# Top-k attention and a gated feed-forward on one core: 144 equal units, one tail transpose, a new order within a unit

## The chip, the cores and the metric

One core of a Trainium2 chip runs the whole program. Times are microseconds on the device, from one execution or, where it is said, the median of several; lower is better. PE is TensorE, DVE is VectorE, ACT is ScalarE, POOL is GpSimd, SP is SyncE, which issues the transfers.

## What is computed

```python
# q, k, v: (8, 8, 576, 64) float32: batch, heads, sequence, head width
scores = (1 / sqrt(64)) * q @ k.transpose(0, 1, 3, 2)
kth = the 32nd largest of each row
scores = where(scores >= kth, scores, -1e9)
attn = exp(scores - max); attn = attn / (sum(attn) + 1e-9)
x = (attn @ v) as 4608 rows of 512
h = x @ w_in                # (4608, 2048)
out = (h * cos(h)) @ w_out  # (4608, 512)
```

All of it is float32. The weights arrive as float64 and are decoded on the chip.

## The kernel before

**Units.** The work of attention is cut into units: one tile of queries of one batch with one pair of heads (`hp`, four pairs). A sequence has 576 rows, four tiles of 128 and a tail of 64. A full unit has 128 queries for each of its two heads, so two score tiles of 128 x 576. A tail unit has 64 queries, and its two heads share the partitions of one tile. There are 128 full and 32 tail units (lines 134 to 143).

**Stages of a unit.** `scores` (L173) multiplies q and k on PE, in two halves of 288 keys for each head, and ACT copies them to `s`. `topk_round` (L201), four times on DVE, takes the eight largest (MAX8) and blots them out (MATCH_REPLACE8). `bounds` (L217, POOL) makes the two limits, `softmax` (L231, ACT) a Prelu that sinks what is below the 32nd value and an Exp that sums into `den`; `reciprocal` (L246) adds epsilon on POOL and divides on DVE; `normalise` (L255) multiplies on POOL. `transpose_main` (L263) turns four tiles of 128 keys for each head, `transpose_tail` (L278) the last 64 keys of each head, with a copy by ACT behind each. `values` (L290) is P@V on PE, the tail's matmul of 64 rows last, and a copy to `xT`.

**Feed-forward.** When all units of a block of tokens are done (256 tokens, 128 at both ends; 20 blocks), `ff1` (L335) multiplies by `w_in` into PSUM, ACT copies to `g`, POOL reduces to one period in four passes (L360 to L363), ACT takes the sine (L373), POOL multiplies (L379), and `ff2` (L382) multiplies by `w_out`. A chunk is a tile of 1,024 columns of `g`; five of them exist (`CHUNKS`).

**The order.** The loop at L445 writes slot i with the top-k of unit i, the softmax of unit i - 1 and the transposes and P@V of unit i - 2; the scores of unit i + 2 are asked for first. `feed` (L404) puts in pieces of the feed-forward by a credit of 2.1 per full unit, at most 4 stored, the second product first if its chunk is gated. A call of `ff1` issues 2,048 moved columns on PE, and one of `ff2` also. A scheduler then orders each engine's instructions by their dependences, so that the rows of an engine need not stand as the code is written. The weights are decoded in the first eight slots, four chunks of 128 x 512 in each.

Of the kernel before, what the change touches and what calls it, by code (L numbers as in the profile page):

```python
# [30 lines left out]
def kernel(  # L31
# [58 lines left out]
    stages = ExitStack()  # L90
    staged = {}

    def load_weights(i):
# [6 lines left out]
        st = stage.tile([P, CW, 2], I32, tag="st", name="st")  # L100
        nc.sync.dma_start(out=st.rearrange("p w i -> p (w i)"), in_=src)
        staged[i] = st

    def decode_weights(i):
# [7 lines left out]
        r = stage.tile([P, CW], I32, tag="lo", name="lo")  # L112
        nc.scalar.mul(out=r, in_=lo.bitcast(U32), mul=2.0**-29)
        sg = stage.tile([P, CW], F32, tag="sg", name="sg")
# [20 lines left out]
    for b in range(B):  # L135
        if b % 2 == 0:
            tiles = [(i * P, P) for i in range(NT)] + [(MAIN, TAIL)]
        else:
            tiles = [(0, TAIL)] + [(TAIL + i * P, P) for i in range(NT)]
        for q0, rows in tiles:  # L140
            for hp in range(NP):
                units.append({"b": b, "hp": hp, "q0": q0, "rows": rows, "tok": b * S + q0})
    NU = len(units)
    pairs = {}

    def load_qk(b, hp):
        if b >= B:
            return
        st = pairs[b, hp] = {}
        for name, src in (("q", qT), ("k", kT)):  # L150
            t = loads.tile([P, S], F32, tag=name, name=name)
            nc.sync.dma_start(
                out=t, in_=src[b, 2 * hp : 2 * hp + 2].rearrange("h d s -> (h d) s")
            )
            st[name] = t

    def load_v(b, hp):
        if b >= B:
            return
        st = pairs[b, hp]  # L160
# [4 lines left out]
        t = loads.tile([TAIL, P], F32, tag="v_tail", name="v_tail", bufs=6)  # L165
        nc.sync.dma_start(out=t, in_=v[b, MAIN:S, cols])
        st["v_tail"] = t

    def head_rows(u, j):
        r0 = j * (P - u["rows"])  # L170
        return slice(r0, r0 + u["rows"])

    def scores(u):  # L173
        st = pairs[u["b"], u["hp"]]
        qs = slice(u["q0"], u["q0"] + u["rows"])
        sc = ps.tile([P, 2, 2, 512], F32, tag="sc", name="sc", bufs=1)
        for h in range(2):
            for j in range(2):
                d = slice(j * D, (j + 1) * D)
                nc.tensor.matmul(  # L180
                    sc[head_rows(u, j), j, h, 0:HS],
                    st["q"][d, qs],
                    st["k"][d, h * HS : (h + 1) * HS],
                    start=True,
                    stop=True,
                )
        s = work.tile([P, 2, S], F32, tag="s", name="s", bufs=5)
        u["s"], u["n"] = s, u["rows"] * 2 // P
        if u["n"] == 2:
            nc.scalar.copy(  # L190
                out=s.rearrange("p j (h w) -> p (j h) w", h=2),
                in_=sc.rearrange("p j h w -> p (j h) w")[:, :, 0:HS],
            )
        else:
            for j in range(2):
                r = head_rows(u, j)
                nc.scalar.copy(
                    out=s[r, 0].rearrange("p (h w) -> p h w", h=2), in_=sc[r, j, :, 0:HS]
                )

    def topk_round(u, rnd):  # L201
        s, n = u["s"], u["n"]
# [6 lines left out]
        for j in range(n):  # L209
            nc.vector.max(m8[:, j, at], src[:, j])  # L210
        if rnd < TOPK // 8 - 1:
            for j in range(n):
# [4 lines left out]
    def bounds(u):  # L217

        n = u["n"]
        nb = small.tile([P, 2, 2], F32, tag="nb", name="nb")  # L220
        nc.gpsimd.tensor_scalar(  # L221
            out=nb[:, 0:n], in0=u.pop("m8")[:, 0:n, 0 : TOPK : TOPK - 1], scalar1=-SCALE,
# [3 lines left out]
        nc.gpsimd.tensor_tensor(  # L226
            out=nd[:, 0:n], in0=nb[:, 0:n, 0], in1=nb[:, 0:n, 1], op=ALU.subtract
        )
        u["nb"], u["nd"] = nb, nd

    def softmax(u):  # L231

        s, n, nb, nd = u["s"], u["n"], u.pop("nb"), u.pop("nd")
        for j in range(n):
# [3 lines left out]
        den = small.tile([P, 2], F32, tag="den", name="den")  # L238
        for j in range(n):
# [4 lines left out]
        u["den"] = den  # L244

    def reciprocal(u):  # L246
        n, den = u["n"], u["den"]
        nc.gpsimd.tensor_scalar(  # L248
            out=den[:, 0:n], in0=den[:, 0:n], scalar1=1.0, scalar2=EPS, op0=ALU.mult, op1=ALU.add
        )  # L250
        rden = small.tile([P, 2], F32, tag="rden", name="rden")
        nc.vector.reciprocal(rden[:, 0:n], den[:, 0:n])  # L252
        u["rden"] = rden

    def normalise(u):  # L255
        s, rden = u["s"], u.pop("rden")
        for j in range(u["n"]):
# [5 lines left out]
    def transpose_main(u):  # L263

        s, n = u["s"], u["n"]
        pT = u["pT"] = work.tile([P, NT, 2, P], F32, tag="pT", name="pT")
        for j in range(n):
            tp = ps.tile([P, NT, P], F32, tag="tp", name="tp")
            for c in range(NT):
                nc.tensor.transpose(tp[:, c], s[:, j, c * P : (c + 1) * P], ident)  # L270
            if n == 2:
                nc.scalar.copy(out=pT[:, :, j], in_=tp)  # L272
            else:
                nc.scalar.copy(
                    out=pT[:, :, :, 0:TAIL], in_=tp.rearrange("p c (j s) -> p c j s", j=2)
                )

    def transpose_tail(u):  # L278
        s, n = u["s"], u["n"]
        pt = u["pT_tail"] = work.tile([TAIL, 2, P], F32, tag="pT_tail", name="pT_tail")  # L280
        tp = ps.tile([P, 512], F32, tag="tp", name="tp")
        for j in range(n):
# [258 lines left out]
```

## Time and profile before

| | us |
|---|---|
| median of 3 runs (1915.38 to 1919.62) | 1918.83 |
| the profiled execution's own time | 1908.91 |
| its span, first to last instruction | 1907.1 |
| PE busy | 1708.2 (90%) |
| DVE busy | 1483.7 (78%) |
| ACT busy | 1232.1 (65%) |
| POOL busy | 953.1 (50%) |

The span is that of one execution with the profiler on. A busy share is an average over the decoding at the start, the steady part and the end, in which DVE has nothing to do. A matmul's end is modelled and takes in the drain of the array, so that several that follow each other read as busy although each waits for another engine in between; the distance from start to start tells more. In a row of the timeline the first number is the start, the second the time from there to the end of the last of the xcount instructions merged in it, and the bracket the idle time of the engine before it and what ended that. Each float32 matmul is two rows of the count.

### The profile page before, as it was taken

Reading aid. Unit: us, or ns where it says so; the run is one execution under the profiler, and the core shown is the slowest. Engines: PE = TensorE matmul, PEld = TensorE weight load, DVE = VectorE, ACT = ScalarE, POOL = GpSimd, SP = SyncE. Lnnn points to the kernel's source line nnn. Section 1 sums busy time; section 2 is a strip of 40 time slices with the busy share of each in tenths; the row PEclk is TensorE's granted clock in tenths of the full one; section 3 lists DMA queues with packets and bytes.
Section 4 is the critical chain, followed back from the end, with each engine's and each line's share of the span. In section 5 each row is a group of like instructions: output and inputs, shape, how many; then the busy total and the mean of one; then the engine's idle time right before and its main releaser. Section 6 shows DMA issues by size and latency. Waiting matters only on the chain.

```text
span 1907.1 us, 26842 instructions
## 1 busy us (share of the span) xinstructions
PE 1708.2 (90%) x9632; PEld 1112.8 (58%) x9632; DVE 1483.7 (78%) x3137; ACT 1232.1 (65%) x2146; POOL 953.1 (50%) x1198
## 2 busy tenths in 40 slices
PE   3658999999899999998999999999999999989995
PEld 2346565656565656656565656565656565656653
DVE  7989889986878679897878868988887868897200
ACT  6776776765757575767676766776766666676511
POOL 5895355544545352636363635563635444554613
PEclk9979999999999999999999999999999999999998
DMA  6420110001000010001100010001000010000000
GB/s 220 133 90 16 48 34 7 7 31 37 25 6 1 32 42 25 1 28 35 37 1 12 13 61 13 12 1 62 19 13 6 6 44 19 7 6 6 7 6 11
DMA packets 38598, 56.26 MB, mean 29 GB/s; under 512 B 3136, under 2 KB 21568, under 8 KB 38464
## 3 DMA queue, kind: packets, MB, share of 16 engines
q1 hardware_dynamic: 38464, 54.54, 8.9%
q8 instruction: 76, 1.25, 0.3%
q14 instruction: 58, 0.48, 0.1%
HBM read 45.09 MB, written 9.44 MB: 29 GB/s over the span
## 4 chain that ended last, share of the span: by engine, by line
DVE 26%; PE 25%; POOL 25%; ACT 19%; issue 4%; DMA 0%; POOLq 0%; SPq 0%; ACTq 0%
DVE m L210 13%; DVE rest L213 11%; PE o L391 10%; POOL x L363 7%; PE mm L348 7%; ACT s L240 4%; POOL x L361 3%; POOL s L258 3%; POOL x L362 3%; POOL x L360 3%; PE o L303 3%; ACT s L235 3%; PE sc L180 3%; ACT x L373 3%; POOL g L379 2%
## 5 line engine op out<-in xcount | busy, mean ns | idle before, releaser
L210 DVE MAX8 m<-rest 128x8 f32<-128x576 f32 x864 | 616.1, 747 | 2.9
L348 PE MATMUL mm<-xT,w_in 128*128 128x256 f32 (+1 forms) x2560 | 551.7, 371 | 27.4 <-ACT g L355 13.9
L391 PE MATMUL o<-w_out,g 128*128 128x512 f32 x1152 | 539.9, 612 | 35.8 <-POOL g L379 35.8
L348 PEld LDWEIGHTS mm<-xT,w_in 128*128 128x128 f32 x2560 | 452.0, 197 | 118.9 <-issue 29.0
L213 DVE MATCH_REPLACE8 rest<-m,rest 128x576 f32<-128x576 f32 x576 | 423.8, 742 | 0.0
L391 PEld LDWEIGHTS o<-w_out,g 128*128 128x128 f32 x1152 | 212.4, 194 | 276.8 <-issue 233.7
L210 DVE MAX8 m<-s 128x8 f32<-128x576 f32 x288 | 205.5, 748 | 164.6 <-ACT s L190 136.4
L235 ACT ACTIVATE s<-s,nb 128x576 f32<-128x576 f32 x288 | 215.4, 772 | 153.5 <-POOL nb L221 153.1
L180 PE MATMUL sc<-k,q 64*128 64x288 f32 (+1 forms) x1280 | 270.4, 461 | 21.9 <-ACT s L190 14.1
L258 POOL TENSOR_SCALAR s<-s,rden 128x576 f32<-128x576 f32 x288 | 215.8, 757 | 132.9 <-DVE rden L252 108.1
L240 ACT ACTIVATE s<-s,nd 128x576 f32<-128x576 f32 x288 | 221.8, 771 | 18.3 <-POOL nd L226 16.3
L248 POOL TENSOR_SCALAR den<-den 128x2 f32<-128x2 f32 (+1 forms) x160 | 31.1, 194 | 362.7 <-ACT s L240 353.4
L213 DVE MATCH_REPLACE8 rest<-m,s 128x576 f32<-128x576 f32 x288 | 211.9, 742 | 0.0
L379 POOL TENSOR_TENSOR g<-g,x 128x1024 f32<-128x1024 f32 x72 | 170.1, 2362 | 63.3 <-ACT x L373 62.8
L303 PE MATMUL o<-pT,v 128*64 128x128 f32 (+1 forms) x2560 | 168.5, 276 | 19.6 <-ACT pT L272 12.5
L180 PEld LDWEIGHTS sc<-k,q 64*128 64x128 f32 (+1 forms) x1280 | 128.3, 187 | 87.9 <-issue 31.4
L270 PEld LDWEIGHTS tp<-ident,s 128*128 128x128 f32 x1152 | 136.2, 144 | 70.5 <-issue 38.0
L270 PE MATMUL tp<-ident,s 128*128 128x128 f32 x1152 | 161.1, 280 | 16.6 <-POOL s L258 12.6
L303 PEld LDWEIGHTS o<-pT,v 128*64 128x64 f32 x2560 | 132.0, 141 | 71.5 <-ACT pT L272 30.1
L363 POOL TENSOR_TENSOR x<-g,x 128x1024 f32<-128x1024 f32 x72 | 170.5, 2368 | 1.7
L190 ACT COPY s<-sc 128x1152 f32<-128x1152 f32 x128 | 142.1, 1110 | 38.7 <-PE sc L180 38.4
L272 ACT COPY pT<-tp 128x512 f32<-128x512 f32 x256 | 137.5, 584 | 26.0 <-PE tp L270 25.6
(44 smaller groups left out, 1353.2 us busy)
## 6 DMA issues: line engine op xcount, KB each, us to landing
q<-in_q_dram SPq DMA_DIRECT2D x32, 288.0 KB, 2.8
k<-in_k_dram SPq DMA_DIRECT2D x32, 288.0 KB, 3.2
out_dram<-ob SPq DMA_DIRECT2D x36, 256.0 KB, 2.0
st<-in_moe_w_in_dram SPq DMA_DIRECT2D x16, 512.0 KB, 4.2
v<-in_v_dram SPq DMA_DIRECT2D x32, 256.0 KB, 2.9
st<-in_moe_w_out_dram SPq DMA_DIRECT2D x16, 512.0 KB, 3.5
v_tail<-in_v_dram SPq DMA_DIRECT2D x32, 32.0 KB, 2.6
```

Source lines behind the costliest of these rows:

```text
L180: nc.tensor.matmul(sc[head_rows(u, j), j, h, 0:HS], st["q"][d, qs], st["k"][d, h * HS : (h + 1) * HS], start=True, stop=True,)
L210: nc.vector.max(m8[:, j, at], src[:, j])
L213: nc.vector.match_replace(rest[:, j], m8[:, j, at], src[:, j], NEG)
L235: nc.scalar.activation(out=s[:, j], in_=s[:, j], func=AF.Prelu, bias=nb[:, j, 1:2], scale=SCALE, alpha=FAR)
L240: nc.scalar.activation(out=s[:, j], in_=s[:, j], func=AF.Exp, bias=nd[:, j : j + 1], scale=1.0, accum_out=den[:, j : j + 1],)
L258: nc.gpsimd.tensor_scalar(out=s[:, j], in0=s[:, j], scalar1=rden[:, j : j + 1], scalar2=1.0, op0=ALU.mult, op1=ALU.mult,)
L270: nc.tensor.transpose(tp[:, c], s[:, j, c * P : (c + 1) * P], ident)
L303: nc.tensor.matmul(o[d, 0:w], lhsT, rhs, start=c == 0, stop=c == NT)
L348: nc.tensor.matmul(mm[:, a * w : (a + 1) * w], w_in[f // FC][:, c, (f % FC) * P : (f % FC + 1) * P], blk["xT"][:, c], start=c == 0, stop=c ...
L363: gp.tensor_tensor(out=x, in0=g, in1=x, op=ALU.subtract)
L379: nc.gpsimd.tensor_tensor(out=g, in0=g, in1=x, op=ALU.mult)
L391: nc.tensor.matmul(o, g[:, at : at + P], w_out[f], start=f == 0, stop=f == NF - 1)
```

## The change

**Units** become 144 equal ones of 128 rows of the flattened tokens, each with a list of parts: where a tile straddles two batches (4 tiles, 16 units) scores and P@V are issued once for each part. **The last keys of both heads**: k of the second head is loaded turned by 64 keys (its last 64 first), so that the first head's last 64 columns and the second head's first 64 lie side by side in `s`; one transpose of 128 columns turns both, one copy takes them, and v's tail is a 128 x 128 tile with one head's rows in each diagonal quarter and zeros elsewhere. **The order of a slot**: P@V comes before the scores of unit i + 2, both after the third round; the reciprocal stands behind the fourth round, its epsilon behind the second; normalising moves to the next slot's start. **Feed-forward pieces** are half as large (a call of `ff1` or `ff2` issues 1,024 moved columns), with a credit of 4.2 per unit, at most 6 stored. **Staging** of the weights uses the buffers of the feed-forward. **Loads** are issued at slots worked out from each buffer's last use. **At the end**, when no unit is left (`ff["end"]`), DVE reduces to one period in two passes and multiplies by the sine.

```diff
+    for t0 in range(0, B * S, P):
+        parts = []
+        for i, a in enumerate((t0, t0 + TAIL)):
+            b, q0 = a // S, a % S
+            if parts and parts[-1][0] == b:
+                parts[-1][2] = P
+            else:
+                parts.append([b, q0, TAIL, i * TAIL])
...
+        nc.sync.dma_start(out=t[0:D], in_=kT[b, 2 * hp])
+        nc.sync.dma_start(out=t[D:P, TAIL:S], in_=kT[b, 2 * hp + 1, :, 0:MAIN])
+        nc.sync.dma_start(out=t[D:P, 0:TAIL], in_=kT[b, 2 * hp + 1, :, MAIN:S])
...
+                k0 = j * TAIL + c * P
+                nc.tensor.transpose(tp[:, c], s[:, j, k0 : k0 + P], ident)
...
+        s = u.pop("s").rearrange("p j k -> p (j k)")
+        nc.tensor.transpose(tp[:, 0:P], s[:, MAIN : MAIN + P], ident)
+        nc.scalar.copy(out=pt, in_=tp[:, 0:P])
...
+        if ff["end"]:
+            nc.vector.tensor_scalar(
+                out=x, in0=g, scalar1=0.25, scalar2=MAGIC, op0=ALU.add, op1=ALU.add
+            )
+            nc.vector.scalar_tensor_tensor(
+                out=x, in0=x, scalar=MAGIC, in1=g, op0=ALU.subtract, op1=ALU.subtract
+            )
+            waiting.append((blk, g, x, ff["now"], -TWO_PI_BELOW))
+            return
...
+            eng = nc.vector if ff["end"] else nc.gpsimd
+            eng.tensor_tensor(out=g, in0=g, in1=x, op=ALU.mult)
...
-        for f in range(f0, f0 + 4):
+        for f in range(f0, f0 + 2):
...
+        ff["credit"] = min(ff["credit"] + 4.2, 6.0)
         ff["now"] += 1
-        if i + 2 < NU:
-            scores(units[i + 2])
         if w:
             bounds(w)
-        gates()
+        if x:
+            normalise(x)
         if u:
             topk_round(u, 0)
         decode(1)
         if w:
             softmax(w)
-        sines(2)
-        if credit >= 1 and feed():
-            credit -= 1
+        gates()
+        feed(2)
+        if x:
+            transpose_main(x)
         if u:
             topk_round(u, 1)
         decode(1)
+        feed(1)
+        if x:
+            transpose_tail(x)
+        feed(6)
         if w:
-            reciprocal(w)
-            normalise(w)
+            add_eps(w)
+        sines(2)
         if u:
             topk_round(u, 2)
         decode(1)
         if x:
-            transpose_main(x)
-        while credit >= 1 and feed():
-            credit -= 1
-        if x:
-            transpose_tail(x)
             values(x)
+        if i + 2 < NU:
+            scores(units[i + 2])
         if u:
             topk_round(u, 3)
+        if w:
+            reciprocal(w)
         decode(1)
```

PE, a steady unit before (`mm` first product, `tp` transposes, `o` P@V, `sc` scores):

```order
L348 MATMUL mm<-xT,w_in_80 128x256 x8
L270 MATMUL tp<-ident,s 128x128 x8
L348 MATMUL mm<-xT,w_in_80 128x256 x8
L283 MATMUL tp<-ident,s 64x128 x2
L303 MATMUL o<-pT,v 64x128 x8
L303 MATMUL o<-pT_tail,v_tail 64x128 x2
L180 MATMUL sc<-k,q 128x288 x4
```

and in the changed program a unit with four pieces, then one with half a piece (`o_6591` is the second product's):

```order
L334 MATMUL mm<-xT,w_in_81 128x256 x8
L264 MATMUL tp<-ident,s 128x128 x8
L334 MATMUL mm<-xT,w_in_82 128x256 x4
L272 MATMUL tp<-ident,s 128x128
L334 MATMUL mm<-xT,w_in_82 128x256 x4
L289 MATMUL o<-pT,v 64x128 x8
L289 MATMUL o<-pT_tail,v_tail_112 64x128 x2
L184 MATMUL sc<-k,q 128x288 x4
```

```order
L264 MATMUL tp<-ident,s 128x128 x8
L391 MATMUL o_6591<-w_out_96,g 128x512
L272 MATMUL tp<-ident,s 128x128
L184 MATMUL sc<-k,q 128x288
L289 MATMUL o<-pT,v 64x128 x8
L289 MATMUL o<-pT_tail,v_tail_106 64x128 x2
```

Half of a feed-forward block that stood between transposes and tail now stands between the tail and P@V; the second piece shows a unit in which the feed had almost nothing to give.

DVE, a steady unit, before and in the changed program (`m` the largest values, `rest` what is left of the scores):

```order
L210 MAX m_4286<-s 128x8 x2
L213 MATCH_REPLACE rest<-m_4286,s 128x576 x2
L210 MAX m_4286<-rest 128x8 x2
L213 MATCH_REPLACE rest<-m_4286,rest 128x576 x2
L252 RECIPROCAL rden<-den 128x2
L210 MAX m_4286<-rest 128x8 x2
L213 MATCH_REPLACE rest<-m_4286,rest 128x576 x2
L210 MAX m_4286<-rest 128x8 x2
```

```order
L206 MAX m_4448<-s 128x8 x2
L209 MATCH_REPLACE rest<-m_4448,s 128x576 x2
L206 MAX m_4448<-rest 128x8 x2
L209 MATCH_REPLACE rest<-m_4448,rest 128x576 x2
L206 MAX m_4448<-rest 128x8 x2
L209 MATCH_REPLACE rest<-m_4448,rest 128x576 x2
L206 MAX m_4448<-rest 128x8 x2
L246 RECIPROCAL rden<-den 128x2
```

The reciprocal has moved from between two rounds to the end of the unit.

DVE at the end of the changed program, behind the last top-k, the first two of eleven chunks:

```order
L206 MAX m_12781<-rest 128x8 x2
L246 RECIPROCAL rden<-den 128x2 x2
L350 TENSOR_SCALAR x<-g 128x1024
L353 SCALAR_TENSOR_TENSOR x<-x,g 128x1024
L379 TENSOR_TENSOR g<-g,x 128x1024
L350 TENSOR_SCALAR x<-g 128x1024
L353 SCALAR_TENSOR_TENSOR x<-x,g 128x1024
L379 TENSOR_TENSOR g<-g,x 128x1024
```

Before, these passes stood on POOL, five to a chunk, for all 72 chunks.

## Rows read from the trace of the kernel before

**Rows 1.** The page, busy time of each engine, share of the span, instructions.

```profile
PE 1708.2 (90%) x9632; PEld 1112.8 (58%) x9632; DVE 1483.7 (78%) x3137; ACT 1232.1 (65%) x2146; POOL 953.1 (50%) x1198
```

**Rows 2.** Timeline of DVE in a steady stretch: first MAX8 of units.

```profile
900.37 1.42 DVE L210 MAX8 m<-s 128x8 f32<-128x576 f32 x2 [4.02 <-ACT s L190]
910.74 1.42 DVE L210 MAX8 m<-s 128x8 f32<-128x576 f32 x2 [0.57 <-ACT s L190]
920.40 1.40 DVE L210 MAX8 m<-s 128x8 f32<-128x576 f32 x2
...
998.01 1.42 DVE L210 MAX8 m<-s 128x8 f32<-128x576 f32 x2 [3.76 <-ACT s L190]
```

**Rows 3.** Groups of DVE from 902 to 998.5: busy, mean ns, idle before, releaser.

```profile
L210 DVE MAX8 m<-s 128x8 f32<-128x576 f32 x15 | 10.7, 750 | 11.6 <-ACT s L190 11.6
L252 DVE RECIPROCAL rden<-den 128x2 f32<-128x2 f32 x8 | 1.3, 160 | 7.4 <-POOL den L248 7.4
```

**Rows 4.** Timeline of PE, matmuls, 1738 to 1755.

```profile
1738.39 0.38 PE L283 MATMUL tp<-ident,s 128*64 128x128 f32 x2
1738.70 1.09 PE L303 MATMUL o<-pT,v 128*64 128x128 f32 x16
1739.72 0.44 PE L303 MATMUL o<-pT_tail,v_tail 64*64 64x128 f32 x4
1740.09 1.24 PE L180 MATMUL sc<-k,q 64*128 64x288 f32 x8
1741.26 3.72 PE L348 MATMUL mm<-xT,w_in 128*128 128x256 f32 x16
1744.82 1.04 PE L270 MATMUL tp<-ident,s 128*128 128x128 f32 x8
1745.69 3.62 PE L348 MATMUL mm<-xT,w_in 128*128 128x256 f32 x16
...
1754.13 0.44 PE L303 MATMUL o<-pT_tail,v_tail 64*64 64x128 f32 x4 [1.82 <-ACT pT_tail L284]
```

**Rows 5.** Groups by form, whole span: waits that the tail units have their share in.

```profile
L210 DVE MAX8 m<-s 128x8 f32<-128x576 f32 x288 | 205.5, 748 | 164.6 <-ACT s L190 136.4 <-ACT s L197 28.2
...
L252 DVE RECIPROCAL rden<-den 128x1 f32<-128x1 f32 x32 | 5.0, 156 | 40.3 <-POOL den L248 40.2
```

**Rows 6.** Timeline of DVE: the ninth unit's first MAX8, the last unit's last.

```profile
146.44 0.76 DVE L210 MAX8 m<-s 128x8 f32<-128x576 f32 x1
...
1778.83 1.41 DVE L210 MAX8 m<-rest 128x8 f32<-128x576 f32 x2
```

**Rows 7.** Stretches: length, busy PE, PEld, DVE, ACT, POOL, granted clock, DMA share, GB/s.

```profile
900.00:998.00 98.00, 92.31 (x499) 60.95 (x498) 78.62 (x168) 64.68 (x112) 47.33 (x60) 0.97 0.06 18
...
1893.50:1904.00 10.50, 9.59 (x16) 3.90 (x16) 0.00 (x0) 0.60 (x1) 0.13 (x1) 0.75 0.00 0
```

**Rows 8.** Timeline of PE at the end, behind the last P@V and the last matmuls.

```profile
1820.04 14.00 PE L391 MATMUL o<-w_out,g 128*128 128x512 f32 x32
...
1893.68 9.59 PE L391 MATMUL o<-w_out,g 128*128 128x512 f32 x16 [10.10 <-POOL g L379]
```

**Rows 9.** Groups by form, whole span: prices of single operations.

```profile
L213 DVE MATCH_REPLACE8 rest<-m,rest 128x576 f32<-128x576 f32 x576 | 423.8, 742 | 0.0
L240 ACT ACTIVATE s<-s,nd 128x576 f32<-128x576 f32 x288 | 221.8, 771 | 18.3 <-POOL nd L226 16.3
L379 POOL TENSOR_TENSOR g<-g,x 128x1024 f32<-128x1024 f32 x72 | 170.1, 2362 | 63.3 <-ACT x L373 62.8
L373 ACT ACT_TABLE_LOAD x67 | 86.0, 1283 | 1.2
L355 ACT ACTIVATE g<-mm 128x512 f32<-128x512 f32 x144 | 84.2, 586 | 100.4 <-PE mm L348 100.3
L373 ACT ACTIVATE x<-x,halfpi 128x1024 f32<-128x1024 f32 x72 | 82.7, 1148 | 86.4 <-POOL x L363 86.2
L119 DVE TENSOR_SCALAR w_in<-w_in x16: 401/417/761, 12.2 to 72.0; 128x512 f32<-128x512 f32 x16
```

More of the change, by code (lines that the diff above doesn't have):

```diff
@@ L179, in scores @@
                 d = slice(j * D, (j + 1) * D)
[L180 to L199, printed above, removed]
+                for b, q0, rows, r0 in u["parts"]:
+                    st = pairs[b, u["hp"]]
+                    nc.tensor.matmul(
+                        sc[r0 : r0 + rows, j, h, 0:HS],
+                        st["q"][d, q0 : q0 + rows],
+                        st["k"][d, h * HS : (h + 1) * HS],
+                        start=True,
+                        stop=True,
+                    )
+        s = u["s"] = work.tile([P, 2, S], F32, tag="s", name="s", bufs=5)
+        nc.scalar.copy(
+            out=s.rearrange("p j (h w) -> p (j h) w", h=2),
+            in_=sc.rearrange("p j h w -> p (j h) w")[:, :, 0:HS],
+        )
     def topk_round(u, rnd):
-        s, n = u["s"], u["n"]
+        s = u["s"]
         if rnd == 0:
@@ L237, in softmax @@
             )
-        den = small.tile([P, 2], F32, tag="den", name="den")
-        for j in range(n):
+        den = u["den"] = small.tile([P, 2], F32, tag="den", name="den")
+        for j in range(2):
             nc.scalar.activation(
@@ L243, in softmax, with add_eps @@
             )
-        u["den"] = den
-    def reciprocal(u):
[L247 to L253, printed above, removed]
+    def add_eps(u):
+        den = u["den"]
+        nc.gpsimd.tensor_scalar(
+            out=den, in0=den, scalar1=1.0, scalar2=EPS, op0=ALU.mult, op1=ALU.add
+        )
+    def reciprocal(u):
+        u["rden"] = small.tile([P, 2], F32, tag="rden", name="rden")
+        nc.vector.reciprocal(u["rden"], u.pop("den"))
     def normalise(u):
         s, rden = u["s"], u.pop("rden")
-        for j in range(u["n"]):
+        for j in range(2):
             nc.gpsimd.tensor_scalar(
@@ L263, in transpose_main @@
     def transpose_main(u):
-        s, n = u["s"], u["n"]
+        s = u["s"]
         pT = u["pT"] = work.tile([P, NT, 2, P], F32, tag="pT", name="pT")
-        for j in range(n):
+        for j in range(2):
             tp = ps.tile([P, NT, P], F32, tag="tp", name="tp")
             for c in range(NT):
[L270 to L276, printed above, removed]
+                k0 = j * TAIL + c * P
+                nc.tensor.transpose(tp[:, c], s[:, j, k0 : k0 + P], ident)
+            nc.scalar.copy(out=pT[:, :, j], in_=tp)
@@ L393, in ff2 @@
             )
-        if f0 + 4 < NF:
+        if f0 + 2 < NF:
             return
@@ L441, in decode @@
                 ff["weights"] += 1
-    per_batch = NU // B
-    credit = 0.0
+    last = {}
+    for i, u in enumerate(units):
+        for part in u["parts"]:
+            last[part[0], u["hp"]] = i
+    at_slot = {}
+    order = [(b, hp) for b in range(B) for hp in range(NP)]
+    for load, bufs, behind in ((load_qk, 5, -1), (load_v, 6, 3)):
+        for n in range(NP, len(order)):
+            slot = last[order[n - bufs]] + behind if n >= bufs else 2
+            at_slot.setdefault(slot, []).append((load, *order[n]))
+    load_qk(0, 0)
+    load_weights(0)
+    load_qk(0, 1)
+    load_weights(1)
+    scores(units[0])
+    for hp in range(2, NP):
+        load_qk(0, hp)
+    for hp in range(NP):
+        load_v(0, hp)
+    scores(units[1])
     for i in range(NU + 2):
+        ff["end"] = i >= NU
         u = units[i] if i < NU else None
```

203 lines of the change are left out of this document (83 added, 120 removed).

## The prediction

> **What bounds the kernel now.** I read the shares of busy time first, then the DVE timeline of one steady stretch, then PE's timeline beside it, then the two ends of the program.
>
> The shares say PE 90%, DVE 78% [rows 1], which looks like a matmul-bound kernel. The steady stretch says otherwise. On DVE a unit's top-k that waits for nothing takes 9.66 us from first MAX8 to first MAX8 (910.74 to 920.40), and 0.15 more with a reciprocal in it, less what overlaps: 9.7. Eight units, 900.37 to 998.01, took 97.6 us, 12.2 each [rows 2]. The idle time of DVE in that stretch is 7.4 us before the reciprocal, which waits for POOL's `den`, and 11.6 before the first MAX8 of a unit, which waits for ACT's copy of the scores [rows 3]; with 8 x 9.7 = 77.6 they make 96.6 of the 97.6.
>
> PE's own need comes from starts, since a matmul's end is modelled and its drain counts as busy. From start to start [rows 4]: tail transposes 0.31, P@V 1.02, its tail 0.37, scores 1.17, transposes 0.87; together 3.74 a unit. A matmul is two rows here. I count feed-forward in pieces of 1,024 moved columns (4 matmuls of 256 in the first product or 2 of 512 in the second; one call of the changed kernel, half a call before): sixteen rows of the first product take 3.56 us from start to start [rows 4], so a piece 1.78; 32 rows of the second took 14.00 [rows 8], so 1.75. At 1.77 there are 576 of them, 4 per unit. Eight units ask PE for 8 x 3.74 + 32 x 1.77 = 86.6 us, 11 less than they took. PE and DVE both wait: PE stops for 1.82 us before P@V's tail [rows 4], then the scores come late, then DVE stands still.
>
> **The change part by part.**
>
> Equal units. 128 full and 32 half units become 144 full ones; the top-k work is the same (288 tiles of 128 rows). The half units' own waits on DVE were 28.2 us for their scores and 40.3 for `den` [rows 5], 68 us that have no place any more; they fall under the pace below. The 16 units that straddle two batches issue twice the scores and P@V matmuls, exactly as many as the half units did: nothing on PE.
>
> One tail transpose instead of two, and a copy of 128 columns instead of 256: at most 0.31 - 0.11 = 0.2 us on PE a unit (a transpose among eight costs 0.87/8 = 0.11), leaving 3.54. I take 3.6. P@V's tail has the same columns; a contraction of 128 rows half full of zeros costs no column more.
>
> Loads. Per pair of heads and batch, k comes in three transfers and the tail of v in two: 3 more issues x 32 pairs on SP's queue, which issues transfers and nothing else, and the output's 36 stand behind them. A load is issued at least a unit before its first use, and two output buffers turn over in several units, so I cost it at nothing; without that cover scores of a straddling unit, or ACT's output copy, would wait.
>
> Order within a unit. The reciprocal now stands behind all four rounds, and `den`'s addition is issued a round earlier. On DVE the next unit's MAX8 is queued behind the reciprocal, so it must not be late: from the end of the top-k, four ACT passes of 0.77, a table load of 1.28 [rows 9] and the small steps on POOL, for which I allow 0.8, come to 5.2 us, against 9.7 available. So the 7.4 us per eight units go. Normalising moves to the next unit's start, on POOL between bounds and their difference, while ACT has its two Prelu; transposes follow two pieces (3.5 us), so they find it done.
>
> Smaller pieces. Between transposes and tail, and between tail and P@V, one piece each now covers ACT's copy. PE's waits inside a unit should shrink; the total of columns stays. But the changed order has a catch that I counted in it: five chunk buffers hold four chunks of a block and one of the next, and with credits capped at 6 feeding repeats every **nine** units: 0.5, 5.5, 4, 4, 4, 4, 5.5, 3.5, 1 pieces, 32 in all, where attention asks for 36. The backlog grows: behind the last P@V stand 75.5 pieces (32 before), and 88 behind the last top-k.
>
> Pace. Nine units need 9 x 3.6 + 32 x 1.77 = 89.0 us of PE and 9 x 9.7 = 87.3 of DVE. The floor is 9.9 a unit. The ceiling is the old waste kept: (97.6 + 9.7) / 9 = 11.92. Between them: the seven full units hold 30.5 pieces, 7 x 3.6 + 30.5 x 1.77 = 79.2 on PE against 67.9 on DVE, an excess of 11.3. Scores are made two units ahead, but the softmax stands behind the copy of the scores on ACT, so I let 5 us of it be absorbed; the two thin units run at DVE's pace. 87.3 + 6.3 = 93.6, and 0.3 us a unit for waits between PE and ACT: 96.3, **10.7 to 10.8**. I take 10.75, nearer the floor because the two named waits are what the new order removes. POOL is next: two passes of 2.36 us [rows 9] and three shorter ones fall to it in a unit with a chunk, beside normalising.
>
> The end. Before, the last 16 rows wait 10.10 us for one chunk's chain [rows 8]. On DVE the chain has three passes over 1,024 columns. The trace has no such pass: 0.83 would be twice the 512-column TENSOR_SCALAR's 417 ns, 2.36 is POOL's; I take 1.3, the 742 ns of MATCH_REPLACE8 over 576 columns scaled [rows 9], since it is plain DVE work. With ACT's copy and sine the chain is 0.58 + 2.6 + 1.15 + 1.3 = 5.6. [...] Between the two ends of the rows (0.83 and 2.36) the eight waits below move by 11 us down and 25 up; both stay in the range. After the last top-k: 88 x 1.77 = 156, two units' transposes and P@V 5, seven chunk waits of 5.6 less two pieces of matmuls, 2 us each, plus a last of 5.6, together 20, and 4 us to the end as now (1903.3 to 1907.1): 185. That is 58 us more than now, when the last top-k ended at 1780.2 [rows 6]; this part alone costs.
>
> Sum for the span: to the ninth unit 146, as now [rows 6], when the weights are decoded (staging now shares buffers with the feed-forward, which may cost or, by the better order, give a few us); nine units with few pieces 9 x 9.7 = 87; 127 x 10.75 = 1365; 185. Together 1783, against 1907.1. The execution's own time was 1.8 over its span, and the median of the runs 9.9 over that: **1795 us**.
>
> **The rivals.**
>
> A, slower: the backlog decides. The nine-unit round keeps all the old waiting, 11.92 a unit, and the end still grows by 58 us: 146 + 87 + 127 x 11.92 + 185 = 1932, with 12 on top 1944. It decides from a pace of 11.72. For it: the chunk buffers are unchanged and five and a half pieces in a unit ask 13.4 us of PE. Against it: the reciprocal's wait is plainly removed.
>
> B: only the reciprocal's 7.4 us per round go, the waits for scores stay: 11.92 - 0.82 = 11.1, 1828, **1840** with 12 on top. For it: ACT's order is still strict and PE still feeds it late in full units.
>
> [...]
>
> D: all waits go and PE's floor holds, 9.9 a unit, 1257 for the 127: 1675, **1687** on the runs.
>
> That the change does not do what it says is a small one: the matmul counts of scores and P@V stay, only 144 transposes (some 20 us) go; if that were all it would be A.
>
> **How the numbers follow.** The forecast's case, 1715 to 1825, has 0.58; B 0.15; C 0.10; D 0.10; A 0.07. No change within 0.2%, about what a measurement here can tell, lies only at A's edge: 0.01 of it. So faster 0.93, same 0.01, slower 0.06. The range runs from 1715, which leaves out most of D, to 1870, which takes in B and C and leaves out A.
>
> **What would show it.** Right: reciprocals with no idle time before them; steady first-MAX8 distances near 9.7 with some of 12 to 13 in rounds of nine units; top-k over near 1600 us; some 185 us of matmuls behind it. Wrong: `den` waits that persist (then POOL's queue), a pace above 11.1 (then ACT or the clock), granted clock under 0.95 in the steady part (C), or waits of PE for k's transfers in the straddling units.

## The result, and the profile after

The changed kernel takes **1833.59 us** (median of 4 runs, 1830.66 to 1836.45) against 1917.13 for the kernel before (4 runs beside it): a ratio of 0.956, 95% interval 0.954 to 0.959. The forecast was 1795 in a range of 1715 to 1870: the sign and the range held, but the time lies above the forecast's own case (to 1825), 6 us from rival B (1840) and 39 from the forecast. The profiled execution took 1836.45 us, 1.75 over its span.

The page of the changed kernel, its span and busy shares (compare [rows 1]):

```profile
span 1834.7 us, 26443 instructions
...
PE 1641.7 (89%) x9488; PEld 1077.8 (59%) x9488; DVE 1503.4 (82%) x3154; ACT 1173.5 (64%) x2056; POOL 854.2 (47%) x1103
```

The changed kernel cut in three stretches: to the first MAX8 of the ninth unit, from there to the last top-k (called the body below), and behind it (the tail). Columns: length; busy PE, PEld, DVE, ACT, POOL; granted clock, DMA share, GB/s.

```profile
0.00:156.80 156.80, 81.42 (x411) 53.96 (x412) 141.60 (x262) 105.42 (x184) 113.85 (x119) 0.83 0.45 138
156.80:1644.90 1488.10, 1392.54 (x8340) 913.61 (x8339) 1326.93 (x2859) 1030.78 (x1815) 736.88 (x978) 0.98 0.07 22
1644.90:1834.70 189.80, 167.76 (x739) 110.27 (x738) 34.85 (x36) 37.31 (x58) 3.45 (x7) 0.98 0.02 9
```

The same stretches of the kernel before, cut at its own ninth unit and last top-k [rows 6]:

```profile
0.00:146.40 146.40, 79.46 (x402) 53.19 (x404) 128.07 (x256) 104.35 (x177) 111.76 (x110) 0.93 0.47 148
146.40:1780.20 1633.80, 1528.36 (x8716) 994.03 (x8713) 1355.40 (x2881) 1102.06 (x1926) 798.76 (x1059) 0.98 0.06 21
1780.20:1907.10 126.90, 100.42 (x520) 65.55 (x518) 0.20 (x2) 25.66 (x43) 42.57 (x31) 0.93 0.02 9
```

The body lost 146 us, the tail gained 63, the start 10. In both kernels PE is busy in 93 to 94% of the body (1392.54 of 1488.10, 1528.36 of 1633.80); the experiments below come back to that.

DVE's waits in the changed kernel (groups by line; the last columns are the idle time before the group and what ended it), against [rows 3, 5]:

```profile
L206 DVE MAX8 m<-s 128x8 f32<-128x576 f32 x288 | 203.4, 746 | 162.4 <-ACT s L192 162.4
...
L246 DVE RECIPROCAL rden<-den 128x2 f32<-128x2 f32 x144 | 21.4, 149 | 13.0 <-POOL den L240 12.9
```

The wait before the reciprocal is nearly gone, 13.0 us over the whole span where the 32 half units alone had 40.3 [rows 5]. The wait for the scores is not smaller: 162.4 against 164.6.

One round of nine units in the steady part of the changed kernel: its last five units, first MAX8 to first MAX8, then the whole round (columns as above). The four units left out take 9.70 each, as the first of these:

```profile
1250.60:1260.30 9.70, 8.54 (x58) 6.59 (x57) 9.70 (x23) 6.06 (x12) 1.99 (x5) 1.00 0.11 30
1260.30:1272.70 12.40, 10.60 (x66) 8.07 (x65) 9.74 (x22) 8.74 (x16) 10.13 (x14) 1.00 0.08 24
1272.70:1285.70 13.00, 12.44 (x76) 9.22 (x75) 9.82 (x22) 10.11 (x18) 10.06 (x11) 1.00 0.09 25
1285.70:1300.00 14.30, 13.59 (x74) 9.75 (x73) 9.84 (x22) 11.40 (x19) 10.65 (x11) 1.00 0.00 1
1300.00:1309.70 9.70, 9.70 (x58) 6.02 (x57) 9.70 (x22) 5.36 (x10) 0.51 (x2) 1.00 0.00 0
1211.80:1309.70 97.90, 92.41 (x527) 60.38 (x526) 87.60 (x191) 68.69 (x121) 49.16 (x65) 1.00 0.13 40
```

Six of the nine units go at DVE's own pace, 9.70. Three, those with pieces of the first product, take 12.4 to 14.3. Set the last row beside the first of [rows 7]: there eight units, with PE busy 92.31 of 98.00; here nine, with PE busy 92.41 of 97.90. As many us of PE now carry one unit more (the feed brings 32 pieces in either, by the count in the prediction). The granted clock of this round is 1.00: its thin units cost no clock.

Where ScalarE stands in such a round (timeline of ACT; in brackets the idle time before, and what ended it):

```profile
1279.19 1.28 ACT L372 ACT_TABLE_LOAD   x1
1282.85 1.15 ACT L372 ACTIVATE x<-x,halfpi 128x1024 f32<-128x1024 f32 x1 [2.37 <-POOL x L362]
1283.90 0.58 ACT L344 ACTIVATE g<-mm 128x512 f32<-128x512 f32 x1
1284.38 0.26 ACT L294 COPY xT<-o 128x128 f32<-128x128 f32 x1
1284.53 1.13 ACT L192 COPY s<-sc 128x1152 f32<-128x1152 f32 x1
```

ScalarE stands 2.37 us before Sin, whose operand POOL has not finished; the copies of g and of the scores stand behind it, and the next unit's MAX8 starts as the scores' copy ends. That looks like the cause of the 162 us, and it was my theory for the first two sets of runs.

PE's groups of the same kind in the kernel before, busy and idle time:

```profile
L348 PE MATMUL mm<-xT,w_in 128*128 128x256 f32 (+1 forms) x2560 | 551.7, 371 | 27.4 <-ACT g L355 13.9 <-ACT xT L308 13.5
...
L303 PE MATMUL o<-pT_tail,v_tail 64*64 64x128 f32 (+1 forms) x640 | 69.4, 295 | 54.6 <-ACT pT_tail L284 54.4
L283 PE MATMUL tp<-ident,s 128*64 128x128 f32 x288 | 60.0, 282 | 19.2 <-ACT pT L272 18.9
```

and in the changed kernel:

```profile
L334 PE MATMUL mm<-xT,w_in 128*128 128x256 f32 (+1 forms) x2560 | 551.3, 366 | 44.5 <-ACT g L344 40.3 <-ACT xT L294 4.0
...
L264 PE MATMUL tp<-ident,s 128*128 128x128 f32 x1152 | 163.9, 282 | 40.0 <-POOL s L251 40.0
L289 PE MATMUL o<-pT_tail,v_tail 128*64 128x128 f32 (+1 forms) x640 | 62.6, 271 | 0.4 <-ACT pT_tail L273 0.4
L272 PE MATMUL tp<-ident,s 128*128 128x128 f32 x144 | 44.4, 308 | 55.8 <-ACT pT L265 50.3 <-DMA v<-in_v_dram 5.4
```

### The profile page after: what moved, and what is told of

It is laid out like the page before. It is cut to its first block, busy times and chain, and to the rows that moved or that the text cites. A ratio compares the mean times of both kernels' runs of the same rounds, so it can differ in the third digit from the quotient of the medians.

```text
span 1834.7 us, 26443 instructions
## 1 busy us (share of the span) xinstructions
PE 1641.7 (89%) x9488; PEld 1077.8 (59%) x9488; DVE 1503.4 (82%) x3154; ACT 1173.5 (64%) x2056; POOL 854.2 (47%) x1103
## 4 chain that ended last, share of the span: by engine, by line
DVE 52%; ACT 17%; POOL 15%; PE 12%; issue 3%; DMA 1%; SPq 0%; POOLq 0%; ACTq 0%
DVE m L206 27%; DVE rest L209 22%; PE o L391 6%; POOL x L362 5%; PE mm L334 4%; ACT s L228 4%; ACT s L233 3%; ACT x L372 3%; ACT s L192 2%; POOL x L359 2%; POOL x L361 2%; POOL x L360 2%; ACT L233 2%; ACT g L344 2%; PE o L289 1%
## 5 line engine op out<-in xcount | busy, mean ns | idle before, releaser
L334 PE MATMUL mm<-xT,w_in 128*128 128x256 f32 (+1 forms) x2560 | 551.3, 366 | 44.5 <-ACT g L344 40.3
L391 PE MATMUL o<-w_out,g 128*128 128x512 f32 x1152 | 539.7, 606 | 22.2 <-POOL g L379 11.5
L334 PEld LDWEIGHTS mm<-xT,w_in 128*128 128x128 f32 x2560 | 440.1, 193 | 142.8 <-ACT g L344 66.6
L391 PEld LDWEIGHTS o<-w_out,g 128*128 128x128 f32 x1152 | 207.8, 193 | 243.3 <-issue 217.3
L206 DVE MAX8 m<-s 128x8 f32<-128x576 f32 x288 | 203.4, 746 | 162.4 <-ACT s L192 162.4
L184 PE MATMUL sc<-k,q 64*128 64x288 f32 (+1 forms) x1280 | 239.6, 455 | 24.7 <-ACT s L192 15.3
L216 POOL TENSOR_SCALAR nb<-m 128x4 f32<-128x4 f32 x144 | 29.6, 205 | 381.9 <-DVE rden L246 370.6
L192 ACT COPY s<-sc 128x1152 f32<-128x1152 f32 x144 | 160.7, 1116 | 53.3 <-PE sc L184 52.2
L265 ACT COPY pT<-tp 128x512 f32<-128x512 f32 x288 | 154.3, 582 | 44.6 <-PE tp L264 44.6
L184 PEld LDWEIGHTS sc<-k,q 64*128 64x128 f32 (+1 forms) x1280 | 115.1, 184 | 84.3 <-issue 37.3
L344 ACT ACTIVATE g<-mm 128x512 f32<-128x512 f32 x144 | 84.5, 587 | 125.2 <-PE mm L334 125.1
L379 POOL TENSOR_TENSOR g<-g,x 128x1024 f32<-128x1024 f32 x61 | 144.5, 2370 | 28.4 <-ACT x L372 25.1
```

What stands on the lines that cost most here:

```text
L184: nc.tensor.matmul(sc[r0 : r0 + rows, j, h, 0:HS], st["q"][d, q0 : q0 + rows], st["k"][d, h * HS : (h + 1) * HS], start=True, stop=True,)
L192: nc.scalar.copy(out=s.rearrange("p j (h w) -> p (j h) w", h=2), in_=sc.rearrange("p j h w -> p (j h) w")[:, :, 0:HS],)
L334: nc.tensor.matmul(mm[:, at : at + w], w_in[f // FC][:, c, (f % FC) * P : (f % FC + 1) * P], blk["xT"][:, c], start=c == 0, stop=c == NC - 1,)
L391: nc.tensor.matmul(o, g[:, at : at + P], w_out[f], start=f == 0, stop=f == NF - 1)
```

## The experiments

Every edit is made to the changed kernel; times are medians of 4 runs (10 for the equal units alone). The first set undoes parts of the change, and tries the theory of Sin. The kernel before ran again beside each set, and its median moved by 2 us (1915.19 to 1917.13). The changed kernel did not, so little hangs on a difference of a few us from its 1833.59.

**The reciprocal back behind round 1.**

```diff
         if w:
             add_eps(w)
+            reciprocal(w)
+            normalise(w)
         sines(2)
```

(and their calls at the end of the unit and at its head are taken out)

> The changed kernel with the reciprocal and the normalise put back where they stood, behind round 1 of the same unit (the addition of EPS stays on GpSimd just ahead of them). Theory (the gain is the VectorE wait for the denominator, 132 us before and 13 us now): the wait comes back, 100 to 135 us of it before RECIPROCAL, and the time goes to 1910 to 1960 us. Rival (the gain is the equal units and the order of P@V and scores, and the reciprocal's place only shows where VectorE happens to wait): the wait before RECIPROCAL comes back but the wait before the first MAX8 (162 us) falls by as much, and the time stays at 1825 to 1850 us.

1866.79 us, 33 more than the changed kernel; against before 0.974 (0.972 to 0.976). Between both expectations. DVE in this run:

```profile
L206 DVE MAX8 m<-s 128x8 f32<-128x576 f32 x288 | 203.8, 748 | 145.0 <-ACT s L192 145.0
...
L246 DVE RECIPROCAL rden<-den 128x2 f32<-128x2 f32 x144 | 23.1, 160 | 71.1 <-POOL den L240 70.8
```

58 us of wait come back before the reciprocal, 17 go before the scores, and only 33 show in the time. In the kernel before, DVE stands 132.6 us there in all:

```profile
L252 DVE RECIPROCAL rden<-den 128x2 f32<-128x2 f32 (+1 forms) x160 | 25.4, 159 | 132.6 <-POOL den L248 132.4
```

Put back here, the old place is worth a quarter of that.

**The feed-forward in pairs of pieces.**

```diff
-                    second.popleft()
-                    ff2(blk, i, f)
-                    n, ff["credit"] = n - 1, ff["credit"] - 1
+                    for _ in range(2):
+                        ff2(*second.popleft())
+                    n, ff["credit"] = n - 2, ff["credit"] - 2
```

(the same for the first product; both conditions ask for two pieces)

> The changed kernel with the feed-forward pieces of the kernel before: two small pieces are always issued together (2,048 moved columns), so the slot of one piece between the main and the tail transposes issues none. Theory (in the three units of a round that carry first products VectorE waits because ScalarE stands behind its Sin, whatever the size of a piece): within 15 us of 1834, 1820 to 1850. Rival (the small pieces let the transposes and the scores pass sooner): 1860 to 1900 us, with VectorE waits in units that carry second products too, where there are none now.

1837.02 us, 3 more, and the waits are the same (162.0 before the first MAX8). The size of a piece hardly matters.

**The end on GpSimd.**

```diff
-        ff["end"] = i >= NU
+        ff["end"] = False
```

> The changed kernel with the reduction and the gate of the last chunks on GpSimd, as everywhere else. Theory: the stretch from the last top-k to the end, 190 us, grows by what GpSimd's chain of a chunk takes more than VectorE's, some 4 to 5 us for each of about 8 chunks on which TensorE waits, so 20 to 45 us: 1855 to 1880 us. Rival (75 pieces of 1.77 us stand there, so TensorE has work beside the chain): under 10 us more, 1834 to 1844.

1878.04 us, 44 more, as the theory had it. The tail of this run, and PE's last wait in it (timeline of PE):

```profile
1644.00:1875.40 231.40, 177.34 (x739) 113.27 (x737) 0.23 (x2) 37.66 (x58) 89.41 (x62) 0.91 0.02 7
```

```profile
1861.85 9.49 PE L391 MATMUL o<-w_out,g 128*128 128x512 f32 x16 [10.09 <-POOL g L379]
```

The tail is 231.4 us in place of 189.8. PE waits nine times for POOL's g there, 40.9 us in all (1.3 to 10.09 each); with the end on VectorE it waits four times, 10.0 in all. That is 31 of the 42 us; 9.6 are PE's own rows, which take longer (177.34 against 167.76) at a granted clock of 0.91 where it was 0.98.

**Sin a unit later in the program.**

```diff
-        ready = [c for c in waiting if c[3] < ff["now"]]
+        ready = [c for c in waiting if c[3] + 1 < ff["now"]]
```

> The changed kernel with one condition changed: a chunk's Sin is asked for two units after its reduction was issued, not one. Theory (the 162 us before the first MAX8 come from ScalarE, which stands in order behind a Sin whose operand GpSimd has not made yet, 67 us of idle time before it, with the copies of the scores and of g behind it): the idle time before Sin falls under 20 us, the wait before the first MAX8 to 60 to 110 us, the time to 1770 to 1800 us. Rival 1 (TensorE's own columns in the units with first products set the pace): the idle time before Sin goes, the wait before MAX8 stays at 150 to 170 us and the time at 1825 to 1845. Rival 2 (chunks come free a unit later and the feed-forward backlog grows): the steady part is shorter, the tail longer by as much or more, 1830 to 1860.

1841.25 us, 8 more, and the idle time before Sin did not fall (76.0 us for POOL's x, 67.3 in the changed kernel). The edit missed its aim: the order on an engine is made when the program is built, and ScalarE's order came out nearly as it was. In 50 of 72 chunks no copy of scores stands between the second copy of g and Sin, in the changed kernel and in this run. So the second set forces it.

**Sin tied behind the copy of the scores.**

```diff
+            nc.scalar.activation(
+                out=bias, in_=u["s"][:, 0, 0:1], func=AF.Identity, bias=halfpi, scale=0.0
+            )
...
-            nc.scalar.activation(out=x, in_=x, func=AF.Sin, bias=halfpi, scale=scale)
+            nc.scalar.activation(out=x, in_=x, func=AF.Sin, bias=bias, scale=scale)
```

(called behind `scores(units[i + 2])`)

> The changed kernel with Sin tied behind the copy of the scores: its bias comes from a one-column ScalarE instruction that reads the scores of the unit after next, with scale 0, so that on ScalarE's order that copy stands ahead of Sin (unlike the run before, in which only the place in the program moved, and ScalarE's order stayed). Theory (VectorE's 162 us before the first MAX8 are ScalarE standing in Sin's wait for GpSimd, with the scores' copy behind it): the idle time before Sin falls from 67 us to under 15, the wait before the first MAX8 from 162 us to 30 to 80, the time to 1730 to 1790 us. Rival (TensorE's own work, or its waits for free buffers, sets the pace of the units with first products): the idle time before Sin goes, the wait before MAX8 stays over 130 us, the time within 1815 to 1850.

1869.44 us, 36 more. ACT and DVE in this run:

```profile
L378 ACT ACTIVATE x<-x,bias 128x1024 f32<-128x1024 f32 x61 | 67.0, 1141 | 1.1 <-POOL x L362 0.7
```

```profile
L206 DVE MAX8 m<-s 128x8 f32<-128x576 f32 x288 | 203.9, 748 | 165.1 <-ACT s L192 165.1
```

The wait before Sin is gone, and so are half of the table loads before it (33 in place of 62), and DVE waits for its scores as long as ever. **The theory fell here.** The rival's waits came, but not its time (1815 to 1850): the run isn't a clean one, for it makes the gate late. PE waits 49.0 us for POOL's g where it waited 11.5, which is near the 36 us; that it makes them isn't shown, for other waits of PE moved too (before the scores 45.8 us where it was 24.7, before the tail's transpose 19.1 where it was 55.8).

**GpSimd's reduction in three passes, and in two.**

```diff
-        gp.tensor_scalar(out=x, in0=g, scalar1=1.0, scalar2=0.25, op0=ALU.mult, op1=ALU.add)
-        gp.tensor_scalar(out=x, in0=x, scalar1=1.0, scalar2=MAGIC, op0=ALU.mult, op1=ALU.add)
+        gp.tensor_scalar(out=x, in0=g, scalar1=0.25, scalar2=MAGIC, op0=ALU.add, op1=ALU.add)
```

> The changed kernel with GpSimd's reduction in three passes, the two additions in one instruction. If that instruction takes as long as one with a multiplication and an addition (1.05 us), a chunk's chain is 1.1 us shorter. Theory (the loop of a slow unit runs through GpSimd's reduction, Sin and the copies behind it): each of some 45 slow units is shorter by 0.6 to 1.1 us, 25 to 50 us in all, 1785 to 1810 us. Rival (GpSimd's reduction lies beside other work): within 10 us, 1824 to 1844.

> The changed kernel with two of GpSimd's four passes left out (the rounding to whole turns, away from the end), so what is gated is not the cosine of the reference. A chunk's chain is 2.2 us shorter. Theory: 50 to 100 us less, 1735 to 1785 us. Rival as in the run with three passes: within 10 us of 1834.

Three passes: 2034.24 us, 200 **more**. The two additions in one instruction cost more than two instructions (groups of POOL in this run; the old form took 1045 to 1048 ns a pass):

```profile
L359 POOL TENSOR_SCALAR x<-g 128x1024 f32<-128x1024 f32 x61 | 222.1, 3641 | 128.1 <-ACT g L344 126.7 <-ACT lo_sg L115 1.4
```

Two passes, without the second and third: 1841.32 us, 8 more. A chain 2.2 us shorter gains nothing, with POOL busy 728.0 us in place of 854.2, so at its present length POOL's chain doesn't seem to set the pace. ScalarE's order changed with it, though: in 69 of 72 chunks no copy of scores stands before Sin, where it was 50.

With three passes the chain is 1.5 us longer (3.64 for 2.1), over 61 chunks 94 us if each pays it once, so by itself it isn't the 200. PE's wait for ACT's g goes from 40.3 to 102.5 us; ScalarE's order changed (64 of 72 chunks); and the granted clock fell. This is the body of that run:

```profile
161.20:1843.70 1682.50, 1478.72 (x8327) 967.41 (x8326) 1330.57 (x2859) 1033.73 (x1814) 827.80 (x919) 0.93 0.07 20
```

The body has 194 us more, which is nearly all of the difference. PE's rows in it, as many as in the changed kernel but for 13, take 86 us longer, at a granted clock of 0.93 where it was 0.98. The three weren't separated.

**Scores asked for at the unit's head.**

```diff
         ff["now"] += 1
+        if i + 2 < NU:
+            scores(units[i + 2])
...
-        if i + 2 < NU:
-            scores(units[i + 2])
```

> The changed kernel with the scores asked for at the head of the unit, as before the change, rather than behind P@V of the same unit. Theory (the scores' place in the program moves only who goes first on TensorE, and VectorE waits for ScalarE): within 12 us of 1834, 1822 to 1846. Rival (P@V ahead of the scores is a part of the gain, or its opposite): 15 to 60 us away on either side, by the wait before the first MAX8.

1839.26 us, 6 more; 151.3 us before the first MAX8 and 21.5 before the reciprocal. P@V ahead of the scores is worth next to nothing.

After these eight, one number had hardly moved whatever ScalarE, POOL or the program order did: the 145 to 169 us before the first MAX8 (but for the long POOL pass), and PE busy in nearly all of the body. So the second theory: PE sets the body, and VectorE's wait is what PE leaves it. The third set takes work from PE alone, and from VectorE alone.

**A quarter of the first product left out.**

```diff
-            for c in range(NC):
+            for c in range(NC - 1):
```

> The changed kernel with a quarter of the first product left out (three of the four blocks of 128 rows of its contraction), so the output isn't the reference's. VectorE, ScalarE and GpSimd do the same work; TensorE does 288 pieces' quarter less, 72 pieces of 1.77 us or 127 us. Theory now (from the body's rows: TensorE is busy in 1,392 of 1,488 us of it whatever the order on ScalarE, VectorE in 1,327): TensorE's own work sets the body, VectorE's wait before the first MAX8 falls from 162 us to under 90, the time to 1720 to 1765 us. Rival (the body is set by a loop of waits through ScalarE and GpSimd, or by VectorE): 1800 to 1840.

**One of four top-k rounds left out.**

```diff
+        if rnd == TOPK // 8 - 1:
+            del u["rest"]
+            return
```

> The changed kernel with the fourth round of top-k left out (24 values are kept, not 32, so the output isn't the reference's). VectorE's work of a unit falls by two MAX8 and two MATCH_REPLACE8 from 9.7 to about 6.6 us, 450 us in all; TensorE's stays. Theory (TensorE sets the body): most of what VectorE saves turns into wait before the first MAX8; the stretch of the weights, in which VectorE is busy 90% and TensorE half, is 20 to 40 us shorter, the body from the ninth unit to the last top-k 0 to 60 us shorter (it can't be under TensorE's 1,392), the time 1740 to 1815 us. Rival (VectorE sets the body): the body falls under 1,392 us because TensorE's pieces are left for the tail, the tail grows, and the time is under 1740 us or the tail over 230 us.

With less on PE 1762.52 us, 71 less. With less on VectorE 1825.05 us, 9 less. The body of the first run, then that of the second:

```profile
152.00:1584.60 1432.60, 1312.19 (x7855) 835.27 (x7855) 1328.22 (x2859) 1031.29 (x1817) 740.51 (x981) 0.97 0.08 23
```

```profile
124.00:1631.10 1507.10, 1401.61 (x8369) 928.18 (x8370) 970.07 (x2054) 1040.40 (x1838) 767.60 (x997) 0.97 0.07 22
```

and DVE's waits in the second:

```profile
L209 DVE MAX8 m<-s 128x8 f32<-128x576 f32 x288 | 204.5, 750 | 309.2 <-ACT s L192 309.2
...
L247 DVE RECIPROCAL rden<-den 128x2 f32<-128x2 f32 x144 | 22.6, 157 | 245.5 <-POOL den L241 245.1
```

VectorE's busy time fell by 390 us (1503.4 to 1113.0) and its waits before MAX8 and the reciprocal grew by 379 (162.4 + 13.0 to 309.2 + 245.5); the body even grew by 19, and only the start, where the weights are decoded on VectorE, shortened (124.0 us to the ninth unit, 33 less). PE's busy time fell by 99 us in the other run (by pieces it was 127), and the time by 71. In the body alone PE is busy 80 us less, and the body is 56 us shorter. VectorE's wait before MAX8 fell to 93.3 there, just over the bound of 90. The first run's time is inside the theory's numbers; the second's is 10 us above, because the body gained nothing at all. So it is PE's work that moves the body, with VectorE close behind: with less on PE it is busy in 1328.22 of 1432.60 us. What the body holds beside PE's work, 95.6 us in which PE stands, no run took away. Of the other two engines, POOL lost 126 us of work in the run with two passes, for no gain; ScalarE lost 66 with Sin tied, but with the late gate, so its work by itself is untried.

**Equal units alone**, with the old order in a unit, the old pieces and the old end.

```diff
         if x:
             transpose_main(x)
+        feed(8)
+        if x:
+            transpose_tail(x)
+            values(x)
```

(all three behind round 2; the pairs of pieces, the reciprocal and the end as in the runs above, the scores at the head, Sin ahead of round 1, the credit's cap at 8 small pieces)

> The equal units, the shared tail and the loads of the changed kernel with the rest of the kernel before: its order in a unit (scores at the head, reciprocal and normalise behind round 1, P@V behind the tail's transpose), its piece size and credit, and its end on GpSimd. Theory (TensorE sets the body, and equal units take 66 us of work from it): 1845 to 1885 us, with the longer backlog's tail and the end on GpSimd (44 us by the run with that end) in it; without these two it would be near the changed kernel. Rival (the reciprocal's move was the gain, as the prediction had it): 1900 to 1960 us, with 100 us or more before RECIPROCAL.

1915.05 us against 1915.63: 0.9995, interval 0.998 to 1.001. Nothing. The theory's time is missed: PE is busy 1690.4 us, 18 less than before and not 66. The time is in the rival's range, but the wait before the reciprocal, 72.9 us, is not. The body and the tail, then PE before P@V's tail, and DVE before the first MAX8, in this run:

```profile
152.00:1796.60 1644.60, 1508.46 (x8601) 993.45 (x8601) 1334.95 (x2862) 1060.95 (x1844) 790.01 (x1012) 0.97 0.07 20
1796.60:1915.10 118.50, 92.86 (x472) 58.76 (x471) 0.20 (x2) 25.57 (x42) 39.10 (x29) 0.89 0.03 9
```

```profile
L289 PE MATMUL o<-pT_tail,v_tail 128*64 128x128 f32 (+1 forms) x640 | 68.4, 296 | 73.2 <-ACT pT_tail L273 73.2
```

```profile
L206 DVE MAX8 m<-s 128x8 f32<-128x576 f32 x288 | 203.9, 747 | 261.1 <-ACT s L192 261.1
```

PE stops before every P@V tail, since nothing stands between the tail's transpose and P@V: 73.2 us here, 54.4 before, 0.4 in the changed kernel. On DVE 60 us of wait go before the reciprocal (132.6 to 72.9), and 97 more stand before the first MAX8, so the half units' waits of [rows 5] are not saved. The tail is 118.5 us, no longer than before: the longer backlog doesn't come with the equal units. Nor does it go with the pairs of pieces, the reciprocal's old place or the scores' (tails of 192.0, 189.9 and 196.9 us). That leaves the feed's place in the unit and the cap on its credit, 8 small pieces here as before the change, 6 in the changed kernel; the two weren't separated.

**Six chunk buffers.**

```diff
-    CHUNKS, XB = 5, 3
+    CHUNKS, XB = 6, 3
```

> The changed kernel with six chunk buffers in place of five, so that the first product of the next block need not stop for chunks. Theory (TensorE sets the body): pieces move from the tail into the body, which grows by as much as the tail falls, and the time stays within 12 us of 1834. Rival (the prediction's account, in which the body has room for the four pieces in 36 that each round leaves behind): 20 to 60 us less, 1775 to 1815.

1848.17 us, 15 more. Its body and tail:

```profile
151.00:1731.00 1580.00, 1451.86 (x8564) 958.57 (x8565) 1330.74 (x2860) 1056.25 (x1843) 776.28 (x1005) 0.98 0.07 21
1731.00:1846.60 115.60, 105.05 (x516) 68.46 (x514) 18.40 (x19) 26.42 (x43) 9.89 (x11) 0.96 0.03 10
```

The tail falls by 74 us, the body grows by 92 and the start loses 6. The pieces do move, and the body has no room for them, as the theory said; its bound of 12 was slightly too tight. PE waits 80.8 us for pT before the tail's transpose, where it waited 50.3.

## Why the prediction was right, and where not

| term of the sum | predicted | measured | difference |
|---|---|---|---|
| to the ninth unit | 146 | 156.8 | +10.8 |
| nine units with few pieces | 87 | 88.6 | +1.6 |
| 127 units | 1365 (10.75 each) | 1399.5 (11.02 each) | +34.5 |
| behind the last top-k | 185 | 189.8 | +4.8 |
| from the span to the median | +11.7 | -1.1 | -12.8 |

The last line is luck: the 9.9 us that I put between the profiled execution and the median, from one execution of the kernel before, did not come again. The span itself came out 52 us over its sum (1834.7 against 1783), and 12.8 of them were given back.

**The pace** is the term that missed most. Of the excess of 11.3 us in the units with many pieces I "let 5 us of it be absorbed", and took a value "nearer the floor because the two named waits are what the new order removes". Only one of them went. The scores' wait takes 10.3 us in the round shown (units of 12.4, 13.0 and 14.3), and of fourteen rounds the first took 89.4 us and the others 97.9 to 105.5, on average (1399.5 - 9.7) / 14 = 99.3, where the sum had 96.75; the round shown is one of the shortest. Top-k was over at 1645 us and not near 1600. Rival B, in which the waits for the scores stay, was worked out at 11.1 a unit, and 11.02 came. That its number is met is in part luck: it takes 0.82 us a unit for the reciprocal's wait, 104 us over the 127, and putting the reciprocal back cost 33.

**The account of VectorE's waits** was wrong beneath the number. I read PE's 90% as no bound, because from start to start eight units ask for 86.6 of 97.6 us. But PE's stops were not refilled with other work, and in the body it is the engine whose work moves the time: 390 us less on VectorE gave 9, and none of them in the body; 99 us less on PE gave 71. So the 7.4 us before the reciprocal in each eight units, counted whole, are 33 us when put back alone, and the equal units, counted with the half units' 68 us, gave nothing by themselves.

**The parts:** undone alone, end on VectorE 44 us, reciprocal's place 33, order of P@V and scores 6, small pieces 3; equal units by themselves 0. They sum to 87 or so, and the kernels are 83.5 apart; parts of one loop need not add up, so that the sum fits is no proof of it. The 44 us were measured with the long tail that the change itself makes (231.4 us with POOL's end, where the kernel before had 126.9); what the new end gives to a short tail no run shows.

**The end** came nearly as counted. The backlog is there and the last top-k ends 63 us further from the end than before. Six chunk buffers move it back, for no gain. VectorE's passes over 1,024 columns took 694 ns (one input) and 1226 and 1225 ns (two), 3.15 us a chunk in place of the 3.9 taken: the scaled MATCH_REPLACE8 was near for two inputs and nearly twice too long for one. Four waits of PE remain, 1.5 to 1.7 us and a last of 5.18, where I had seven of 2 and a last of 5.6: 10.0 in place of 20.

**The smaller pieces** matter less than I thought (3 us). With a piece between the tail's transpose and P@V, PE's 54.4 us of waiting there went, but they did not leave PE: 50.3 us now stand before the tail's transpose (18.9 before) and 40.3 before the first product (13.9). What that place is worth alone no run shows.

**The loads**, put at nothing, cost little: PE waits 9.4 us for k's transfers (7.8 before) and 5.4 for v's. P@V's tail over 128 rows, half of them zeros, took 272 ns (median of its rows), over 64 rows 269 before.

**Rival C**, a granted clock under 0.95 in the steady part, did not come: granted 1.00 in the round shown and 0.98 in the body, as before. No run shows what a lower clock would cost a thin unit: those of that round took 9.70 us each at 1.00. At the end the clock did fall. After a wait of 5.18 us PE's last 16 rows took 9.27 us, at a granted clock of 0.77 (1821.3 to 1830.6), where 16 rows had taken 7.13 at 1.00 (1805.4 to 1812.6):

```profile
1805.45 7.13 PE L391 MATMUL o<-w_out,g 128*128 128x512 f32 x16 [1.54 <-DVE g L379]
...
1821.33 9.27 PE L391 MATMUL o<-w_out,g 128*128 128x512 f32 x16 [5.18 <-DVE g L379]
```

In the run with three passes PE stands 204 us in the body, where it stood 96, and 0.93 was granted; what lowered it there wasn't shown. **Rival A** (11.92 a unit) and **D** (9.9) lie well off.

**Open:** the 10.8 us at the start. The trace shows where they stand: VectorE's decoding passes in that stretch take 70.5 us (94 of them), before the change 56.3 (88), with the same shapes. Why they take longer isn't shown; with six buffers, which the decoding shares, the start is 6 us shorter, and with the scores at the head, which touches no buffer, 5. Staging apart from the chunks wasn't tried. Nor was a third buffer for the transposes, on which PE's largest remaining wait (50.3 us) may rest. No run beat the changed kernel with its whole work.

## What to carry to other kernels

Before a wait on an engine is counted as time, ask which engine's work moves the end: take work from one engine at a time. A busy share of 90% with short stops between may be the bound although a wait elsewhere is larger, when other work doesn't fill the stops (here PE, busy 94% of the body with 95.6 us of stops, beside the 162.4 us for which VectorE waits for its scores). And look at the built order of an engine, not at the program's: a step moved in the program may stay where it was, as Sin did (50 of 72 chunks in both orders).

## What the runs showed of the hardware

On GpSimd a TENSOR_SCALAR over 128x1024 float32 with a multiplication by 1 and an addition took 1045 ns in the changed kernel (mean of 61); with two additions, in the run with three passes, it took 3641 (mean of 61), more than three of the others together. On VectorE the two-addition form of the same size took 694 ns in the changed kernel (mean of 11):

```profile
L350 DVE TENSOR_SCALAR x<-g 128x1024 f32<-128x1024 f32 x11 | 7.6, 694 | 123.2 <-ACT g L344 123.2
```

With the swap from four passes to three the whole kernel was 11% slower than the changed one (2034.24 against 1833.59); ScalarE's order and the granted clock changed with the longer pass, and their shares weren't told apart.
